# Moving the transposes of q, k and the attention output from TensorE to the DMA crossbar, from the tenth pair of heads on

## The chip, the cores and the metric

The kernel runs on one core of one Trainium2 chip. The metric is the device time of one execution in microseconds. Several executions of each kernel are timed beside executions of the kernel before on the same chip. Each "profile" is the trace of one execution ("span" is its length inside the core, about 2 us less than its device time).

Words used below: the TensorE clock of a window is the share of full speed that the trace shows as granted. The DMA share is the sum of the packets' times over the time of the core's 16 DMA engines; it can pass 1. SP's queue issues most transfers of the mid-run. SBUF holds the program's tiles; PSUM is the memory that it gives TensorE to write to.

## The reference, cut to what matters

```python
# attention: q, k, v are (8 batches, 8 heads, 576 tokens, 64), s is (8, 8, 576)
scores = q @ k.T / 8
cum    = cumsum(max(s, 0))
scores = where(causal, -1e9, scores + min(-(cum_i - cum_j), 0))
x      = softmax(scores) @ v               # heads joined: (4608 tokens, 512)
# feed-forward
h   = x @ w_in                             # (4608, 2048)
out = (h * clip(h + 3, 0, 6) / 6) @ w_out  # (4608, 512)
```

## The kernel before

Work goes by *pairs* of heads: 32 pairs, four to a batch. For each pair q and k are loaded, cast to 16 bits by GpSimd and turned, so that the 64 head dimensions lie on the partitions. TensorE does this with an identity matrix, into PSUM; VectorE copies q out, ScalarE copies k:

```python
def transpose(p, i):                       # i = 0: q, 1: k
    ...
    for e in range(6):
        nc.tensor.transpose(pt[:, 96*e : 96*(e+1)], tok[:, i, e]..., ident[0:96, 0:96])
    copy = (nc.vector.tensor_copy, nc.scalar.copy)[i]
    for hh in range(2):
        copy(out=qk[0:64, hh, i, 0:SEQ]..., in_=pt[64*hh : 64*hh + 64, 0:SEQ]...)

def transpose_x(p):                        # the attention output, for the feed-forward part
    ...
    for t in range(5):
        nc.tensor.transpose(pt[:, 128*t : 128*(t+1)], x[:, t]..., ident)
    nc.vector.tensor_copy(out=xT[:, hp, b*SEQ : (b+1)*SEQ], in_=pt[:, 0:SEQ])
    x_done[0] = p + 1                      # readiness, at build time
```

The program fixes at build time in which order each engine gets its instructions. Between the pieces of a pair's attention the program puts *groups* of four feed-forward matmuls, so that TensorE has work while ScalarE computes exponentials. A pair has eight such slots. What goes into a slot is decided when the program is built: a group of the first matmul (`m1`) may stand there only if its block's batch is ready, a group of the second (`m2`) only with some distance to the first.

```python
def m1_ready():
    return (512 * m1_list[done[1]][0] + 511) // SEQ < x_done[0] // PPB      # cut
def m2_ready():
    ...
    return done[1] >= max(need + 2, i + LAG)                               # LAG = 14
...
scores(p, 0, 0); transpose(p + 1, 0); group()                              # pair p > 4
scores(p, 0, 1); av(p - 1, 1, 0);     group()
scores(p, 0, 2); av(p - 1, 1, 1); norm(p - 1, 1); group()
corner(p); transpose(p + 1, 1);       group()
scores(p, 1, 0);                      group()
scores(p, 1, 1); av(p, 0, 0); transpose_x(p - 1); group()
scores(p, 1, 2);                      group()
av(p, 0, 1); norm(p, 0);              group()
```

The groups left over follow after the last pair (the tail).

The softmax here doesn't subtract the row's maximum and nothing guards it: scores larger than these inputs give would overflow.

## Time and profile before

| | kernel before |
|---|---|
| median of three runs | 394.0 us (391.74 to 394.42) |
| span of the profiled run | 391.0 us |
| TensorE busy | 92% |
| VectorE, ScalarE, GpSimd busy | 65%, 64%, 33% |

In mid-run TensorE's busy time equals the window's length, so its queue is the clock of the kernel there; the other figures only say who has room. The prediction shows these lines.

### The profile page before, as it was taken

The page shows a single profiled execution, that of the slowest core. Times are in us where ns is not written, and L with a number is a line of the kernel's source. Part 1 is how long each engine was busy: PE and PEld are TensorE (multiplying, and loading weights), DVE is VectorE, ACT ScalarE, POOL GpSimd, SP SyncE. Part 2 cuts the span into 40 slices and gives each one's busy share as a digit, 9 for nine tenths or more (in the row PEclk, how much of TensorE's full clock was granted, in tenths as well). Part 3 has the DMA queues.
Part 4 walks back from the last instruction along what each step waited for, and adds up shares of the span by engine and source line. Part 5 has one row for each costly group of instructions (what it writes and reads, how often), then busy time and mean ns, then how long its engine had stood idle before and what let it go on. Part 6 is the DMA issues. An engine that isn't in the chain of part 4 may idle for free.

```text
span 391.0 us, 8380 instructions
## 1 busy us (share of the span) xinstructions
PE 361.5 (92%) x3232; PEld 209.8 (54%) x3232; DVE 256.0 (65%) x518; ACT 249.6 (64%) x437; POOL 130.1 (33%) x218
## 2 busy tenths in 40 slices
PE   1576888899999999999999999999999999999995
PEld 0465555555555555555555555555555544444442
DVE  8557798667776777677767777777677555454441
ACT  5567789767777777777777777777677633433410
POOL 6777876433333333333333333333320000000000
PEclk9998999989999999999999999999999999999999
DMA  7799999904555554444555445364000001101012
GB/s 176 141 237 231 234 226 228 207 11 113 121 123 119 122 121 121 119 122 121 122 120 121 121 119 121 102 139 120 32 29 29 27 29 38 43 29 54 29 54 80
DMA packets 63744, 43.50 MB, mean 111 GB/s; under 512 B 42128, under 2 KB 58784, under 8 KB 63704
## 3 DMA queue, kind: packets, MB, share of 16 engines
q1 hardware_dynamic: 56792, 37.63, 39.5%
q0 software_dynamic: 6272, 4.78, 7.7%
q10 hardware_dynamic: 640, 0.56, 0.5%
q8 instruction: 25, 0.41, 0.5%
q14 instruction: 15, 0.12, 0.1%
HBM read 37.11 MB, written 9.44 MB: 119 GB/s over the span
## 4 chain that ended last, share of the span: by engine, by line
PE 81%; DVE 8%; ACT 4%; DMA 2%; issue 2%; POOL 1%; SPq 1%; POOLq 0%; DVEq 0%
PE po L343 30%; PE ph L323 28%; PE O L268 7%; PE S L226 6%; PE pt L194 4%; PE S L221 3%; DVE gT L332 2%; PE ptx L305 2%; DMA raw<-in_q_dram 2%; ACT tr L331 2%; DVE qk L202 1%; ACT qk L202 1%; DVE P L236 1%; DVE x L291 1%; ACT P L234 1%
## 5 line engine op out<-in xcount | busy, mean ns | idle before, releaser
L332 DVE SCALAR_TENSOR_TENSOR gT<-tr,ph 128x512 f16<-128x512 f32 x144 | 98.8, 686 | 104.3 <-ACT tr L331 104.2
L331 ACT ACTIVATE tr<-ph,bias 128x512 f32<-128x512 f32 x144 | 99.1, 688 | 93.8 <-PE ph L323 92.7
L323 PE MATMUL ph<-xT,w_in_sb 128*128 128x512 f16 x576 | 149.9, 381 | 0.8 <-DVE xT L310 0.8
L343 PE MATMUL po<-w_out_sb,gT 128*128 128x512 f16 x576 | 145.5, 379 | 0.0
L234 ACT ACTIVATE P<-S 128x512 f16<-128x512 f32 x192 | 109.6, 593 | 20.8 <-PE S L226 13.7
L343 PEld LDWEIGHTS <-gT 128*128 128x128 f16 x576 | 51.9, 97 | 46.5
L323 PEld LDWEIGHTS <-w_in_sb 128*128 128x128 f16 x576 | 49.9, 98 | 42.2 <-issue 0.8
L121 POOL DMA_DIRECT2D qk<-aug x62 | 36.5, 590 | 87.8 <-PE S L226 78.1
L167 POOL CAST tok<-raw 96x768 f16<-96x768 f32 x63 | 52.2, 864 | 1.7 <-DMA raw<-in_q_dram 0.8
L226 PE MATMUL S<-qk 68*128 68x448 f16 (+3 forms) x256 | 51.9, 285 | 0.1
L268 PE MATMUL O<-va,P 128*128 128x65 f16 x896 | 49.7, 197 | 2.0 <-DVE x L291 2.0
L202 DVE COPY qk<-pt 64x576 f16<-64x576 f16 x64 | 48.1, 751 | 4.2 <-PE pt L194 3.7
L268 PEld LDWEIGHTS <-P 128*128 128x128 f16 x896 | 41.4, 100 | 16.2 <-DVE x L291 3.4
L194 PE MATMUL pt<-ident,tok 96*128 96x96 f16 x384 | 28.6, 214 | 16.7 <-POOL tok L167 13.3
L202 ACT COPY qk<-pt 64x576 f16<-64x576 f16 x64 | 40.5, 633 | 3.4 <-PE pt L194 2.5
L173 POOL CAST va<-vraw 128x512 f16<-128x512 f32 x32 | 19.6, 613 | 66.8 <-PE O L268 56.2
L226 PEld LDWEIGHTS <-qk 68*128 68x128 f16 x256 | 24.7, 102 | 26.5 <-issue 3.2
L291 DVE TENSOR_TENSOR x<-O,rl 128x320 f16<-128x320 f32 x64 | 31.5, 491 | 2.2
L236 DVE TENSOR_TENSOR P<-P,masks_sb 128x512 f16<-128x512 f16 x64 | 29.2, 456 | 5.1 <-ACT P L234 5.0
L194 PEld LDWEIGHTS <-tok 96*128 96x128 f16 x384 | 21.8, 102 | 18.6 <-POOL tok L167 14.5
L352 DVE TENSOR_SCALAR ob<-po 128x512 f32<-128x512 f32 x36 | 24.8, 690 | 10.2 <-PE po L343 9.5
L221 PE MATMUL S<-qk 128*128 128x128 f16 x256 | 26.1, 227 | 3.6 <-DMA qk<-aug 3.6
(37 smaller groups left out, 159.1 us busy)
## 6 DMA issues: line engine op xcount, KB each, us to landing
raw<-in_q_dram SPq DMA_DIRECT2D x32, 288.0 KB, 4.5
out_dram<-ob SPq DMA_DIRECT2D x36, 256.0 KB, 2.1
raw<-in_k_dram SPq DMA_DIRECT2D x31, 288.0 KB, 4.7
vraw<-in_v_dram SPq DMA_DIRECT2D x64, 128.0 KB, 4.2
w_in_sb<-in_moe_w_in_dram POOLq DMA_DIRECT2D x4, 512.0 KB, 9.9
w_out_sb<-in_moe_w_out_dram POOLq DMA_DIRECT2D x8, 256.0 KB, 9.0
vraw<-in_v_dram SPq DMA_DIRECT2D x32, 32.0 KB, 3.9
qk<-aug POOLq DMA_DIRECT2D x62, 9.0 KB, 3.8
```

The source lines that it names most:

```text
L121: eng.dma_start(out=qks[p % NQK][64:68, hh, :, 0:SEQ], in_=aug[g : g + 1, :, :, :])
L167: eng(out=tok[:, i].rearrange("p t h d -> p h t d"), in_=raws[p % NRAW][:, i])
L194: nc.tensor.transpose(pt[:, 96 * e : 96 * (e + 1)], tok[:, i, e].rearrange("p h d -> p (h d)"), ident[0:96, 0:96],)
L202: copy(out=qk[0:64, hh, i, 0:SEQ].rearrange("p (t e) -> p t e", e=6), in_=pt[r : r + 64, 0:SEQ].rearrange("p (e t) -> p t e", e=6),)
L221: mm(S[:, c], lhsT=kT[:, c], rhs=qT[:, c], start=(j == 0), stop=(j == 3))
L226: mm(S[:, c : c + w], lhsT=kT[0:68, 128 * j : 128 * (j + 1)], rhs=qT[0:68, 128 * (j + 1) : SEQ], start=(c == 0), stop=(c != 0),)
L234: nc.scalar.activation(out=pt[:, c], in_=S, func=AF.Exp, scale=0.125)
L268: mm(o[:, i, :], lhsT=lhsT, rhs=va[:, hh, j, 0:65], **kw)
L323: mm(ph, lhsT=w_in_sb[:, kc, ft * 128 : (ft + 1) * 128], rhs=xT[:, kc, n * 512 : (n + 1) * 512], start=(kc == 0), stop=(kc == NKC - 1),)
L331: nc.scalar.activation(out=tr, in_=ph, func=AF.Relu, bias=bias3[:, 0:1])
L332: nc.vector.scalar_tensor_tensor(out=gTs[n][:, ft, :], in0=tr, scalar=6.0, in1=ph, op0=ALU.min, op1=ALU.mult)
L343: mm(po, lhsT=gTs[n][:, ft, t4 * 128 : (t4 + 1) * 128], rhs=w_out_sb[:, ft, :], start=(ft == 0), stop=(ft == NFT - 1),)
```

## The change

From pair 9 on (pairs are counted from 0), q and k of a pair are transposed by the DMA crossbar, which turns blocks of 128x128 on their way from SBUF to SBUF, out of one 16-bit tile; the attention outputs of pairs 8 to 30 go the same way straight into the feed-forward part's input. TensorE loses the transposes, and the copies out of PSUM go too. For that q and k are loaded 128 tokens to a column of blocks (rows of 256 bytes), and the second head's tokens stand 64 columns on, because 576 tokens are 4.5 blocks of 128. Four VectorE copies per pair spread the transposed blocks over the two heads. Casts and crossbar run one pair further ahead, and a batch's readiness is set nearly one pair later, to give the output time to land.

```diff
+    NPE = 2 * PPB + 1                     # 9: the first pair by the crossbar
...
+    def crossbar_qk(p):
+        J[p] = work.tile([128, 9, 128], F16, tag="jt", name="jt")
+        nc.sync.dma_start_transpose(out=J[p], in_=toks[p])
+    def spread(p, i):                     # two VectorE copies, 64x768 and 64x512
+        ...
+    def crossbar_x(p):
+        nc.sync.dma_start_transpose(out=xT[:, hp, b*SEQ : b*SEQ + 640]..., in_=X.pop(p)...)
...
     for p in range(NP):
+        if NPE <= p + 2 < NP:
+            cast_qk(p + 2, ...)
+            crossbar_qk(p + 2)
...
-            transpose(p + 1, 0)
+            get(0)                        # spread from pair 9 on
...
+        if p > NPE:
+            x_done[0] = p - 1
         scores(p, 1, 0)
...
-            transpose_x(p - 1)
+            (crossbar_x if p >= NPE else transpose_x)(p - 1)
```

More of the change, by code (lines that the diff above doesn't have):

```diff
@@ L42 @@
     NBLK = NT // 512
-    SPAD = 640
+    SPAD = 768
+    NPE = 2 * PPB + 1
     NQK = 3
@@ L77, in keep @@
         return made if n > 1 else made[0]
-    raws = keep("raw", [96, 2, 2, 6, D], F32, NRAW)
+    raws = keep("raw", [128, 24 * D], F32, NRAW)
     vraws = keep("vraw", [128, 2, 5, D], F32, NRAW)
@@ L86 @@
     PCs = keep("PC", [128, 192], F16, 2)
-    xT = keep("xT", [128, NKC, NT], F16)
+    xT = keep("xT", [128, NKC, NT + 64], F16)
     w_in_sb = keep("w_in_sb", [128, NKC, DFF], F16)
@@ L94, with raw6, raw9 @@
     aug = keep("aug", [NHEADS, 4, 2, SEQ], F16)
+    def raw6(p):
+        return raws[p % NRAW][0:96].rearrange("p (i h e d) -> p i h e d", i=2, h=2, e=6)
+    def raw9(p):
+        return raws[p % NRAW][:, 0 : 18 * D].rearrange("p (i t d) -> p i t d", i=2, t=9)
     def load_qk(p, i, eng):
         b, h0 = p // PPB, 2 * (p % PPB)
-        raw, src = raws[p % NRAW], (q, k)[i]
-        eng.dma_start(
-            out=raw[:, i].rearrange("p h e d -> p h (e d)"),
-            in_=src[b, h0 : h0 + 2].rearrange("h (p e) d -> p h (e d)", e=6),
-        )
+        src = (q, k)[i][b, h0 : h0 + 2]
+        if p < NPE:
+            eng.dma_start(
+                out=raw6(p)[:, i].rearrange("p h e d -> p h (e d)"),
+                in_=src.rearrange("h (p e) d -> p h (e d)", e=6),
+            )
+        else:
+            eng.dma_start(
+                out=raw9(p)[:, i],
+                in_=src.rearrange("h s d -> (h s) d").rearrange(
+                    "(t p) d -> p t d", p=128
+                ),
+            )
     def load_v(p, eng):
@@ L121, in load_aug @@
             eng.dma_start(
-                out=qks[p % NQK][64:68, hh, :, 0:SEQ], in_=aug[g : g + 1, :, :, :]
+                out=qks[p % NQK][64:68, hh, :, 64 * hh : 64 * hh + SEQ],
+                in_=aug[g : g + 1, :, :, :],
             )
@@ L163, in cast_qk @@
     def cast_qk(p, eng_q, eng_k):
-        tok = work.tile([96, 2, 6, 2, D], F16, tag="tok", name="tok")
+        tok = work.tile([128, 24 * D], F16, tag="tok", name="tok")
+        if p < NPE:
+            tok = tok[0:96].rearrange("p (i e h d) -> p i e h d", i=2, e=6, h=2)
+            for i, eng in enumerate((eng_q, eng_k)):
+                eng(out=tok[:, i].rearrange("p t h d -> p h t d"), in_=raw6(p)[:, i])
+        else:
+            tok = tok[:, 0 : 18 * D]
+            for i, eng in enumerate((eng_q, eng_k)):
+                eng(
+                    out=tok[:, 9 * D * i : 9 * D * (i + 1)],
+                    in_=raws[p % NRAW][:, 9 * D * i : 9 * D * (i + 1)],
+                )
         toks[p] = tok
-        for i, eng in enumerate((eng_q, eng_k)):
-            eng(
-                out=tok[:, i].rearrange("p t h d -> p h t d"), in_=raws[p % NRAW][:, i]
-            )
     def cast_v(p):
@@ L186, in t_bank @@
         if early[0] and other:
-            return psum.tile([128, SPAD], F16, tag="po", bufs=2, name=name)
-        return psum.tile([128, SPAD], F16, tag="t", name=name)
+            return psum.tile([128, 640], F16, tag="po", bufs=2, name=name)
+        return psum.tile([128, 640], F16, tag="t", name=name)
     def transpose(p, i):
@@ L202, in transpose @@
             copy(
-                out=qk[0:64, hh, i, 0:SEQ].rearrange("p (t e) -> p t e", e=6),
+                out=qk[0:64, hh, i, r : r + SEQ].rearrange("p (t e) -> p t e", e=6),
                 in_=pt[r : r + 64, 0:SEQ].rearrange("p (e t) -> p t e", e=6),
+            )
+    J = {}
+    def crossbar_qk(p):
+        J[p] = work.tile([128, 9, 128], F16, tag="jt", name="jt")
+        nc.sync.dma_start_transpose(out=J[p], in_=toks[p])
+    def spread(p, i):
+        jt, qk = J[p], qks[p % NQK]
+        for par, n in ((0, 3), (1, 2)):
+            c = 9 * i + par
+            r, sl = 64 * (c % 2), c // 2
+            src = jt[r : r + 64, sl : sl + n, :]
+            ap = [list(x) for x in src.ap]
+            ap.insert(1, [256, 2])
+            nc.vector.tensor_copy(
+                out=qk[0:64, :, i, 128 * par : 128 * par + 256 * n].rearrange(
+                    "p h (s two c) -> p h s two c", two=2, c=128
+                )[:, :, :, 0, :],
+                in_=bass.AP(src.tensor, src.offset, ap),
             )
@@ L209, with qk_of @@
     mm = nc.tensor.matmul
+    def qk_of(p, hh):
+        r = 64 * hh
+        return (qks[p % NQK][:, hh, i, r : r + 640] for i in range(2))
     def Pof(p, hh):
@@ L214, in scores @@
     def scores(p, hh, g):
-        qT, kT = qks[p % NQK][:, hh, 0], qks[p % NQK][:, hh, 1]
+        qT, kT = qk_of(p, hh)
         pt = Pof(p, hh)
@@ L242, in corner @@
         for hh in range(2):
-            qT, kT = qks[p % NQK][:, hh, 0], qks[p % NQK][:, hh, 1]
+            qT, kT = qk_of(p, hh)
             mm(
@@ L313, in transpose_x @@
         x_done[0] = p + 1
+    def crossbar_x(p):
+        b, hp = p // PPB, p % PPB
+        nc.sync.dma_start_transpose(
+            out=xT[:, hp, b * SEQ : b * SEQ + 640].rearrange("p (t c) -> p t c", c=128),
+            in_=X.pop(p).rearrange("p t h d -> p (t h d)"),
+        )
     gTs, pos = {}, {}
@@ L411 @@
     for i in range(NQK):
-        nc.vector.memset(qks[i][0:64, :, :, SEQ:SPAD], 0.0)
+        for hh in range(2):
+            r = SEQ + 64 * hh
+            nc.vector.memset(qks[i][0:64, hh, :, r : r + 64], 0.0)
     for t in Ps:
@@ L422 @@
             copy(
-                out=qks[i][64:128, hh].rearrange("p i (t c) -> p i t c", c=128),
+                out=qks[i][64:128, hh, :, 64 * hh : 64 * hh + 640].rearrange(
+                    "p i (t c) -> p i t c", c=128
+                ),
                 in_=stair_sb[64:128, :, None, :].to_broadcast([64, 2, 5, 128]),
@@ L465 @@
         nxt = p + 1 < NP
+        ahead = NPE <= p + 2 < NP
+        if p and p + 1 < NPE:
+            cast_qk(p + 1, nc.gpsimd.tensor_copy, nc.gpsimd.tensor_copy)
+        if ahead:
+            cast_qk(p + 2, nc.gpsimd.tensor_copy, nc.gpsimd.tensor_copy)
+            crossbar_qk(p + 2)
         if p and nxt:
-            cast_qk(p + 1, nc.gpsimd.tensor_copy, nc.gpsimd.tensor_copy)
             cast_v(p + 1)
@@ L471, with get @@
         next_weights(1 if p < 3 else 2 if p < 4 else 3)
+        for m in (p + 3, p + 4):
+            if m < NP and (m < NPE) == (m == p + 3):
+                for i in range(2):
+                    load_qk(m, i, nc.sync)
         if p + 3 < NP:
-            for i in range(2):
-                load_qk(p + 3, i, nc.sync)
             load_v(p + 3, nc.sync)
+        def get(i):
+            if p + 1 < NPE:
+                transpose(p + 1, i)
+            elif nxt:
+                spread(p + 1, i)
         if p < PPB:
@@ L479 @@
             scores(p, 0, 1)
-            if nxt:
-                transpose(p + 1, 0)
+            get(0)
             scores(p, 0, 2)
@@ L488 @@
             scores(p, 1, 0)
-            transpose(p + 1, 1)
+            get(1)
             scores(p, 1, 1)
@@ L507 @@
             scores(p, 0, 2)
-            transpose(p + 1, 0)
+            get(0)
             group()
@@ L512 @@
             scores(p, 0, 0)
-            if nxt:
-                transpose(p + 1, 0)
+            get(0)
             group()
@@ L523 @@
         corner(p)
-        if nxt:
-            transpose(p + 1, 1)
+        get(1)
         group()
+        if p > NPE:
+            x_done[0] = p - 1
         scores(p, 1, 0)
```

## The prediction

> **What bounds the kernel now.** I first read the page's busy shares and slices, then a table of windows, the PE timeline inside one pair, the costliest groups, and the waits of the SP queue.
>
> ```profile
> PE 361.5 (92%) x3232; PEld 209.8 (54%) x3232; DVE 256.0 (65%) x518; ACT 249.6 (64%) x437; POOL 130.1 (33%) x218
> PE   1576888899999999999999999999999999999995
> PEclk9998999989999999999999999999999999999999
> DMA  7799999904555554444555445364000001101012
> ```
>
> TensorE leads. DMA is full in slices 3 to 8, up to about 78 us, then half busy to about 275 us. TensorE's granted clock dips near 80 us. The windows (busy us, then clock, DMA share, GB/s) put numbers on this.
>
> ```profile
> 150.90:191.30 40.40, 40.24 (x390) 23.82 (x389) 28.54 (x61) 29.20 (x52) 14.50 (x24) 1.00 0.47 117
> 305.00:390.00 85.00, 81.97 (x436) 38.27 (x433) 39.02 (x64) 30.22 (x46) 0.00 (x0) 1.00 0.12 44
> 77.50:80.00 2.50, 1.88 (x18) 1.07 (x17) 0.95 (x4) 2.16 (x4) 0.00 (x0) 0.82 0.15 29
> 80.00:82.50 2.50, 2.50 (x14) 1.24 (x13) 1.07 (x4) 1.18 (x2) 1.10 (x2) 0.50 0.00 0
> ```
>
> The first is four pairs (one batch), 10.10 us per pair: columns are TensorE, its weight loads, VectorE, ScalarE, GpSimd. TensorE is busy 40.24 of 40.40 us, VectorE 71%, ScalarE 72%. What TensorE is spared here is time, as long as nobody else becomes slower than it. The last two rows are pair 8, where the order of the program offers no feed-forward matmuls for some slots: TensorE idles a little, and then runs at half clock for 2.5 us.
>
> The timeline of TensorE (start, length, line) shows what a transpose costs there:
>
> ```profile
> 163.77 0.42 PE L194 MATMUL pt<-ident,tok 96*128 96x96 f16 x6
> 164.03 1.03 PE L343 MATMUL po<-w_out_sb,gT 128*128 128x512 f16 x4
> 167.58 0.42 PE L194 MATMUL pt<-ident,tok 96*128 96x96 f16 x6
> 167.83 1.03 PE L323 MATMUL ph<-xT,w_in_sb 128*128 128x512 f16 x4
> 170.25 0.45 PE L305 MATMUL ptx<-ident,x 128*128 128x128 f16 x5
> 170.54 1.03 PE L323 MATMUL ph<-xT,w_in_sb 128*128 128x512 f16 x4
> ```
>
> Matmuls overlap, so the start of the next group counts, not the length: six transposes of q take 0.26 us, six of k 0.25, five of the attention output 0.29. Together 0.80 us per pair, 8% of it.
>
> ```profile
> L202 DVE COPY qk<-pt 64x576 f16<-64x576 f16 x64 | 48.1, 751 | 4.2 <-PE pt L194 3.7
> L202 ACT COPY qk<-pt 64x576 f16<-64x576 f16 x64 | 40.5, 633 | 3.4 <-PE pt L194 2.5
> L310 DVE COPY xT<-ptx 128x576 f16<-128x576 f16 x32 | 14.5, 452 | 1.0 <-PE ptx L305 0.9
> L422 DVE COPY qk<-stair_sb 64x1280 f16<-64x1280 f16 x2 | 2.0, 1018 | 0.4 <-DMA stair_sb<-stair 0.4
> SPq L354 <- DVE ob L352: 230.6, 35, 12.0
> ```
>
> The first three copies go away; the fourth has the form of the new ones. The last line is a wait: the SP queue spends 230.6 us blocked, in order, on the store of the result. It has time to spare, but what stands behind that store waits with it.
>
> **What the Trainium skill says.** "VectorE: DVE Perf Modes", section "The three transpose paths", gives 390 ns for a 128x128 transpose on TensorE and 1309 ns for one by the DMA crossbar. The trace disagrees on the first for a filled pipeline: 0.29 us for five is 58 ns each. So the change trades little TensorE time for much DMA time; it pays only because TensorE is the bound one. "DMA: Bandwidth & Descriptors", section "Latency and other measured facts", has 261 GB/s for a crossbar transpose in one kernel; the trace before holds none. The same page, section "Issuing engines are not separate DMA queues", says that all DMAs share the 16 engines: the 0.47 share is where the crossbar must fit. "Advanced Engine Details and Errata", section "X-Bar Transpose (TRN2)", warns of two transpose streams at once; here all come from SP, so one stream.
>
> **The change part by part.**
> *TensorE.* Pairs 9 to 31 lose their q and k transposes, and the outputs of pairs 8 to 30 theirs: 23 of each. 23 x 0.80 = 18.4 us off the path. Span 391.0 becomes 372.6; the pair goes from 10.10 to 9.30 us.
> *ScalarE.* Loses 2 x 0.633 = 1.27 us per pair: 7.30 - 1.27 = 6.03 of 9.30 us. Not on the path.
> *VectorE.* Loses 2 x 0.751 + 0.452 = 1.95 us. It gains four copies inside SBUF, two of 64x768 and two of 64x512 elements (the second head's tokens included, as the crossbar's chunks are common to both). The stair copy takes 1018 ns for 1280 elements in runs of 128; with about 155 ns fixed (a 128-column mask costs 0.22 us in the timeline, a 512-column one 0.42) it is 0.67 ns per element: 0.67 and 0.50 us, together 2.34. VectorE: 7.13 - 1.95 + 2.34 = 7.5 of 9.30 us, 81%. Not the bound, but with less slack than 71%.
> *GpSimd.* Casts 128x576 in place of 96x768, so shorter; 33% busy; not on the path.
> *DMA.* In 150 to 232 us the trace's packets are, per pair: 1152 of 256 bytes (v) at 23 ns, 384 of 1536 bytes (q, k) at 89 ns, 128 of 2048 bytes (results) at 92 ns. Over 16 engines 1.68 + 2.13 + 0.73 = 4.5 us, the 0.47 of the window. New q and k loads are rows of 256 bytes: 2304 x 23 / 16 = 3.36 us, 1.2 us more. The crossbar moves 9 + 5 blocks of 128x128, 459 KB per pair: at the skill's 261 GB/s an estimate of 1.8 us. Sum 4.5 + 1.2 + 1.8 = 7.5 us of 9.30: 81%. It fits, without much room.
> *Order.* q and k of pair p+2 are now transposed at the top of pair p, so a spread has about 8 us from issue to use. For the output the change sets the readiness of a batch almost one pair later. Followed through the program's order: until pair 11 nothing differs; then the feed-forward work that is ready runs out, and seven slots at the end of pair 12 and in pair 13 stay empty. From pair 14 all 8 are filled again, and the tail does 87 groups in place of 80. The work itself is only moved (a group costs 0.86 us anywhere), but the hole costs what pair 8's does: that pair ran from 73.4 to 82.8 us, 9.3 us, with three groups; its matmul work at full clock is 10.1 - 5 x 0.86 = 5.8 us, so 3.5 us were lost, about half of it to the lower clock. I take 3 us for the new hole, and give back 1 us in pair 8, where TensorE waited for copies of transposes (0.80 and 0.62 us) that are gone.
> *Start.* The crossbar for pair 9 is issued while the DMA engines are still full (slices to 78 us), with one more pair of loads ahead of it. I take 1.5 us of lateness there and 1 us in sum where a batch's first feed-forward block meets its last transposed output.
> Sum: 391.0 - 18.4 + 3 - 1 + 1.5 + 1 = 377.1 us of span, 13.9 less; from the median of 394.0, 380 us.
>
> **The rivals.**
> *DMA becomes the bound.* For it: the loads get 1.2 us longer, and the skill's 1309 ns times 14 is 18 us per pair if blocks do not overlap. Against it: the skill's 261 GB/s, and 1309 ns for a lone block must hold much that is latency. The room is 9.3 - 5.7 = 3.6 us per pair; a crossbar at under 459 KB / 3.6 us = 127 GB/s ends the gain, and at half of that the pair lasts about 13 us and the kernel 391 + 23 x 3 = 460 us.
> *The SP queue or late transposed data become the wait.* SP is in order: transposes wait for casts and for the normalised output, and stores of results wait behind them. If issuing a transpose takes some us, or an output comes late at each batch's start, TensorE stands still some us for each of five batches, and its clock drops after each: 385 to 395 us. For it: SP already waits 230.6 us on the result's store. Against it: that is slack, and use lies most of a pair behind issue.
> *VectorE.* If the new copies run at one element per cycle (the 751 ns copy has 1.04 ns per element beyond its fixed part), they cost 3.3 us and VectorE is at 8.5 of 9.3 us; TensorE would wait here and there, some 0.2 us per pair: 384 us.
>
> **Range and chances.** The 18.4 us are sure, being counted from the timeline; with no hole at all the time would be 375. What is unsure is the crossbar's speed, which no row before shows. About two in three that nothing new binds (375 to 386), one in five that waits eat over half of the gain, one in seven that DMA or SP binds and the kernel is slower. So 380 us, 374 to 396 for 8 in 10; faster 0.66, same 0.20, slower 0.14.
>
> **What would show it.** A step is right if: the pair in mid-run lasts 9.3 us with TensorE near 99%; the new copies last about 0.67 and 0.50 us; 256-byte load packets stay near 23 ns and the DMA share is near 0.8; the slot hole appears in pairs 12 and 13 with a lower clock behind it; the tail starts earlier and has 87 groups. It is wrong if TensorE waits on the spread copies or on DMA in every pair, or if the DMA share stands at 1 past 100 us: then the crossbar's packets were slower than I took them.

## More of the kernel before

One more page line of before is needed for comparison, the count of DMA packets:

```profile
DMA packets 63744, 43.50 MB, mean 111 GB/s; under 512 B 42128, under 2 KB 58784, under 8 KB 63704
```

## The result, and the profile after

The changed kernel took 375.81 us (median of four, 374.26 to 376.71), against 393.86 us (four runs, 391.74 to 394.42). The ratio is 0.955, with a 95% interval of 0.950 to 0.960. Ratios here are the mean time of one kernel's runs over the mean of the other's in the same rounds, so not quite the quotient of the medians. Executions over 1.5% slower than the fastest of the same kernel are left out of the means.

The page of the changed kernel, the same lines as the prediction shows of before:

```profile
PE 343.6 (92%) x2841; PEld 192.5 (52%) x2841; DVE 243.8 (65%) x544; ACT 225.3 (60%) x391; POOL 122.8 (33%) x218
PEclk9997699999999999999999999999999999999999
DMA  8699999999979799979999989798411001010012
DMA packets 150589, 54.01 MB, mean 145 GB/s; under 512 B 137808, under 2 KB 145632, under 8 KB 150552
```

TensorE has 18 us less to do (361.5 to 343.6) and its share of the span is the same 92%: still the bound. The DMA line is what looks dangerous. Half busy in mid-run before, it is now at nine tenths to the end of the attention, with well over twice the packets. The windows by stage (four pairs; the pair with empty slots; pair 8; columns as in the prediction):

```profile
160.59:197.48 36.89, 36.89 (x321) 20.65 (x320) 26.15 (x65) 25.13 (x44) 12.62 (x24) 1.00 0.96 170
116.90:123.70 6.80, 5.59 (x67) 3.34 (x64) 5.69 (x13) 5.48 (x10) 4.99 (x9) 1.00 1.12 195
74.42:81.76 7.34, 5.84 (x66) 3.62 (x65) 5.24 (x13) 4.61 (x9) 4.65 (x9) 1.00 1.39 169
```

In mid-run TensorE is busy in all of 36.89 us, four pairs of 9.22. VectorE is busy 26.15 of 36.89 us, 71%, the same share as before. In pair 13 TensorE idles 1.2 us, and unlike pair 8 of before its clock stays at 1.00. The new operations, and the SP queue's wait:

```profile
L249 DVE COPY qk<-jt 64x768 f16<-64x768 f16 x46 | 17.3, 375 | 0.7
L249 DVE COPY qk<-jt 64x512 f16<-64x512 f16 x46 | 13.2, 287 | 1.0
jt<-tok SPq DMA_TRANSPOSE x23, 3.5
xT<-x SPq DMA_TRANSPOSE x23, 3.4
SPq L415 <- DVE ob L413: 117.2, 33, 8.4
```

The copies take 375 and 287 ns, and VectorE is hardly ever idle ahead of them (0.7 and 1.0 us in 92 copies), so the transposed q and k are there when wanted. A transpose lands 3.4 to 3.5 us after its issue (medians). SP's wait for the result's store fell from 230.6 to 117.2 us, while the issuing of its transfers grew from 119 to 212 us: the slack pays for issuing the transposes.

For a ledger I take the start of each pair, the first score matmul of its first head, from TensorE's timeline of the two traces:

| stage | before, us | after, us | difference | of which |
|---|---|---|---|---|
| to the start of pair 8 | 73.43 | 74.42 | +0.99 | open, see below |
| pair 8 | 9.33 | 7.34 | -1.99 | -0.51 transposes, -1.48 less idling, clock stays up |
| pairs 9 to 11 | 30.05 | 27.67 | -2.38 | 3 x 0.80 transposes |
| pairs 12 and 13 | 20.36 | 14.27 | -6.09 | -1.60 transposes, -6.05 seven groups moved to the tail, -0.32 batch start, +1.88 hole |
| pairs 14 to 30 | 171.60 | 156.78 | -14.82 | -13.60 transposes, -1.28 four batch starts |
| pair 31 and tail | 86.23 | 93.12 | +6.89 | +6.05 seven groups, -0.29 transposes, +1.06 a wait |
| span | 391.00 | 373.60 | -17.40 | |

A group is 0.864 us (four matmuls in the timeline), so pair 13 with its three groups should have taken 9.22 - 5 x 0.864 = 4.90 us; it took 6.77, and that is the 1.88 (with rounding). The first pair of each later batch lasted 10.34 us before, the others 10.02; now all last 9.22.

The first two rows are not settled. Pair 8 began at 73.4 and 73.3 us in the two traces with the start of before (the other is readiness alone, below), and at 74.0 to 75.6 us in nine traces with the changed start (left out: two with a long mask operation, see the copies, and the crossbar from pair 5 on). So the lateness may well belong to the change. But the crossbar is not all of it: the nine were already late at the start of pair 7 (64.2 to 65.6 us, against 64.0 and 63.9), where the first transpose is issued, and the latest of all, at 75.6 us, has q and k on TensorE throughout. The cause stays open. Nor is pair 8's gain steady: the kernel with readiness at once, whose program is the changed one up to there, took 8.67 us for it, at a clock of 0.80. At the start of pair 9 before stood at 82.8 us, the changed kernel at 81.8 and, in its second trace, at 82.3.

### The profile page after: what moved, and what is told of

Its sections match the earlier page's. It is cut to its first block, busy times and chain, and to the rows that moved or that the text cites. A ratio compares the mean times of both kernels' runs of the same rounds, so it can differ in the third digit from the quotient of the medians.

```text
span 373.6 us, 7629 instructions
## 1 busy us (share of the span) xinstructions
PE 343.6 (92%) x2841; PEld 192.5 (52%) x2841; DVE 243.8 (65%) x544; ACT 225.3 (60%) x391; POOL 122.8 (33%) x218
## 3 DMA queue, kind: packets, MB, share of 16 engines
q1 hardware_dynamic: 143640, 48.19, 65.6%
## 4 chain that ended last, share of the span: by engine, by line
PE 83%; DVE 9%; ACT 2%; DMA 2%; issue 2%; POOL 1%; SPq 1%; POOLq 0%; DVEq 0%; ACTq 0%
PE po L404 33%; PE ph L384 30%; PE O L321 7%; PE S L279 7%; PE S L274 3%; DMA raw<-in_q_dram 2%; DVE qk L226 2%; DVE gT L393 1%; PE pt L218 1%; ACT tr L392 1%; ACT P L287 1%; DVE P L289 1%; DVE x L344 1%; DVE qk L249 1%; PE ptx L358 1%
## 5 line engine op out<-in xcount | busy, mean ns | idle before, releaser
L384 PE MATMUL ph<-xT,w_in_sb 128*128 128x512 f16 x576 | 148.3, 379 | 0.1
L287 ACT ACTIVATE P<-S 128x512 f16<-128x512 f32 x192 | 112.1, 595 | 45.1 <-PE S L274 22.5
L404 PEld LDWEIGHTS <-gT 128*128 128x128 f16 x576 | 50.3, 98 | 46.1
L384 PEld LDWEIGHTS <-w_in_sb 128*128 128x128 f16 x576 | 51.2, 98 | 43.9 <-issue 0.4
L197 POOL CAST va<-vraw 128x512 f16<-128x512 f32 x32 | 19.7, 615 | 57.2 <-PE O L321 48.2
L189 POOL CAST tok<-raw 128x576 f16<-128x576 f32 x46 | 30.1, 677 | 11.7 <-DMA jt<-tok 4.1
L249 DVE COPY qk<-jt 64x768 f16<-64x768 f16 x92 | 30.5, 331 | 1.7
L274 PEld LDWEIGHTS <-qk 128*128 128x128 f16 x256 | 20.0, 102 | 16.9 <-issue 4.7
L218 PE MATMUL pt<-ident,tok 96*128 96x96 f16 x108 | 9.6, 242 | 15.5 <-POOL tok L185 12.9
L218 PEld LDWEIGHTS <-tok 96*128 96x128 f16 x108 | 7.6, 119 | 17.3 <-POOL tok L185 14.1
```

The source lines that it names most:

```text
L249: nc.vector.tensor_copy(out=qk[0:64, :, i, 128 * par : 128 * par + 256 * n].rearrange("p h (s two c) -> p h s two c", two=2, c=128)[:, :, ...
L274: mm(S[:, c], lhsT=kT[:, c], rhs=qT[:, c], start=(j == 0), stop=(j == 3))
L287: nc.scalar.activation(out=pt[:, c], in_=S, func=AF.Exp, scale=0.125)
L384: mm(ph, lhsT=w_in_sb[:, kc, ft * 128 : (ft + 1) * 128], rhs=xT[:, kc, n * 512 : (n + 1) * 512], start=(kc == 0), stop=(kc == NKC - 1),)
L404: mm(po, lhsT=gTs[n][:, ft, t4 * 128 : (t4 + 1) * 128], rhs=w_out_sb[:, ft, :], start=(ft == 0), stop=(ft == NFT - 1),)
```

## The experiments

**Theory.** TensorE's queue sets the pace of pairs 9 to 30; the gain is its own time for the transposes, less what the later readiness costs in slots that stay empty. **Rivals.** The gain is the relief of VectorE and ScalarE from copies; the DMA is now at its limit; the later readiness costs more, or is not needed. Twelve kernels were run, in three series. The kernel before had medians of 395.49 us in the first, 392.56 in the second and 393.30 in the third. All results were correct.

### TensorE's time alone, given back

The change with as many transposes of a constant tile on TensorE as there were, never read.

```diff
                 spread(p + 1, i)
+                fake(i)                   # 6 x nc.tensor.transpose(pt, masks[0:96, ...], ident)
...
             (crossbar_x if p >= NPE else transpose_x)(p - 1)
+            fake_x()                      # 5 x nc.tensor.transpose(pt, masks[:, ...], ident)
```

> The change, with TensorE transposing a constant tile as often as it transposed before (6 + 6 + 5 per pair, into PSUM that nobody reads), so only TensorE's time is given back; result unchanged. TensorE theory: mid-run pair back to 10.0 us, 375.8 + 18.4 = 394 us. Rival (relief of VectorE and ScalarE is the gain): under 380 us.

Measured: 392.60 us, ratio 0.9995 (0.993 to 1.006): the gain is gone, to within the interval's 2.5 us, with everything else of the change still in place. A window of four pairs:

```profile
146.98:187.04 40.06, 40.06 (x389) 23.80 (x388) 26.23 (x65) 25.10 (x44) 13.23 (x25) 1.00 1.00 163
```

10.02 us a pair, the pace of before, though VectorE and ScalarE (26.23 and 25.10 us) have only the changed kernel's work.

### The copies alone, given back

The five removed copies run again, in the same form and from PSUM, into scratch, on VectorE and ScalarE.

```diff
+                copy = (nc.vector.tensor_copy, nc.scalar.copy)[i]
+                for hh in range(2):
+                    copy(out=junk[:, i, :]..., in_=keep_pt[0][r : r + 64, 0:SEQ]...)
...
+                nc.vector.tensor_copy(out=junkx, in_=keep_pt[0][:, 0:SEQ])
```

> The change, with the five removed copies out of PSUM executed again on VectorE (2 x 0.75 + 0.45 us per pair) and ScalarE (2 x 0.63) into scratch from pair 9 on, beside the new ones; result unchanged. TensorE theory: VectorE goes from 71% to 92% of a pair and TensorE still sets the pace: 376 to 379 us, pair 9.2 to 9.3 us. Rival: VectorE's time counts, pair 10 us or more, 390 us or more.

Measured: 380.87 us, ratio 0.970 (0.964 to 0.976): 5 us slower than the change, more than the theory's 3 at most, far from the rival's 14 or more. The traces say where (a mid-run window, then TensorE's timeline in pair 13):

```profile
131.19:187.00 55.81, 55.81 (x482) 31.37 (x481) 48.53 (x113) 43.20 (x78) 19.36 (x36) 0.99 0.87 173
126.46 0.42 PE L324 MATMUL O<-va,P 128*128 128x65 f16 x8 [1.67 <-DVE x L347]
127.71 0.38 PE L282 MATMUL S<-qk 68*128 68x320 f16 x2 [0.83 <-ACT P L290]
```

With VectorE at 48.53 of 55.81 us, 87%, TensorE is still busy throughout; pairs 15 to 30 last 9.24 us in place of 9.22. But pair 13 lasts 10.39 us in place of 6.77, at a clock of 0.87: with three feed-forward groups in place of eight there is little to hide VectorE's and ScalarE's work, and TensorE waits for it in the open. So the copies (1.95 us of VectorE, 1.27 of ScalarE a pair) cost 0.02 us a pair from pair 15 on, where the slots are full (0.16 to 0.28 in pairs 9 to 12), and 3.6 us in pair 13, where they are empty; which of the two engines costs it is not told apart. (This trace also holds a pair 6 of 10.80 us, ahead of any changed instruction; a mask operation on VectorE took 1.85 us in it in place of some 0.4. Its cause was not looked for.)

### The two halves of the change, and the readiness alone

q and k only (output by TensorE, readiness at once); output only; and the kernel before with the later readiness.

```diff
 # q and k only
-        if p > NPE:
-            x_done[0] = p - 1
-            (crossbar_x if p >= NPE else transpose_x)(p - 1)
+            transpose_x(p - 1)
 # output only
-    NPE = 2 * PPB + 1
+    NPE = NP                              # q and k always by TensorE
+    NPX = 2 * PPB + 1                     # the output by the crossbar from pair 9
 # readiness only (on the kernel before)
-        x_done[0] = p + 1
+        if p < 8 or p == NP - 1:
+            x_done[0] = p + 1
...
+        if p > 9:
+            x_done[0] = p - 1
```

> The change with the crossbar for q and k alone; the attention output is transposed on TensorE as before and readiness is set at once. If the gain is the TensorE time of the transposes (first theory): 23 x 0.51 us saved = 11.7, and pair 8 about 1.2 us shorter as in the full change; no slots left empty in pairs 12 and 13: 381 us, mid-run pair 9.5 us. If the gain comes from relieving VectorE and ScalarE of the q and k copies (rival): all of it stays, 376 us.

> The crossbar for the attention output alone, from pair 9 on, with the later readiness. TensorE theory: 23 x 0.29 = 6.7 us saved, 1.3 us more at the batch starts (four pairs of 10.34 us become 10.02), against 2 to 3.5 us for the empty slots of pairs 12 and 13: 388 to 390 us. Rival (the copies matter): no gain over the delay alone, 394 us or more.

> The kernel before with nothing but the later readiness of a batch (one pair later from pair 10 on), all transposes on TensorE. If the empty slots cost what the traces show in pair 13 and the batch starts gain 4 x 0.32 us: 394 + 2 to 3.5 - 1.3 = 395 to 396 us, pairs of 10.34 us gone. If readiness is free: 394 us or less.

| kernel | median, us | ratio (95% interval) | mid-run pair, us | pairs 12 and 13, us |
|---|---|---|---|---|
| before | 395.49 | 1 | 10.02 (10.34) | 10.34, 10.02 |
| q and k only | 380.69 | 0.966 (0.959 to 0.973) | 9.50 (9.56) | 9.57, 9.50 |
| output only | 391.96 | 0.996 (0.988 to 1.004) | 9.74 | 8.02, 9.88 |
| readiness only | 397.36 | 1.010 (1.002 to 1.019) | 10.02 | 8.30, 8.81 |
| the change (its own four runs, before 393.86) | 375.81 | 0.955 (0.950 to 0.960) | 9.22 | 7.50, 6.77 |

In brackets the first pair of a batch. The pairs shorten by 0.52 us for q and k and 0.28 for the output, within a hundredth of what the timeline of before gave (0.51 and 0.29). The 10.34 us pairs vanish with the later readiness, whoever transposes; with q and k alone moved, at once ready, 0.06 us of the 0.32 is left. But the later readiness alone makes the kernel about 1% slower. Here are pair 13 of the readiness-only kernel and pair 13 of the output-only kernel, as windows, with one line of the latter's timeline:

```profile
121.01:129.82 8.81, 6.31 (x83) 4.17 (x80) 6.12 (x12) 6.40 (x12) 5.23 (x9) 1.00 0.19 32
```

```profile
121.03:130.91 9.88, 7.54 (x79) 4.52 (x76) 5.87 (x11) 6.51 (x12) 5.94 (x9) 0.83 0.48 109
125.28 0.41 PE L219 MATMUL pt<-ident,tok 96*128 96x96 f16 x6 [2.35 <-DVE qk L227]
```

With all transposes on TensorE the hole costs 8.81 - (10.02 - 5 x 0.864) = 3.1 us; with q and k on TensorE and the output on the crossbar 9.88 - (9.74 - 4.32) = 4.5 us, part of it a lower clock (0.83). In the changed kernel it costs 1.9, since nothing waits there for copies of transposes. The kernel with TensorE's time given back bears this out: its transposes are there, their copies are not, and pair 13 lasts 7.04 us, a hole of 1.3. So the output half alone was worth less than I expected (388 to 390 us), and the crossbar for q and k makes the hole cheaper that the output's readiness opens. In total times the two halves add up to the whole within the intervals.

### The readiness at once, and one slot later

The change with a batch ready as soon as the output's transpose is issued; and one slot after that. The change itself ran again beside the second.

```diff
-        if p > NPE:
-            x_done[0] = p - 1
...
             (crossbar_x if p >= NPE else transpose_x)(p - 1)
+            x_done[0] = p                 # at once
         group()
+        if p >= NPE:
+            x_done[0] = p                 # or here: one slot later
```

> The change with readiness set as soon as the crossbar of the attention output is issued. If the delay is needed: the first feed-forward block of five batches waits on TensorE for a transfer that takes 3.4 us to land plus its issue, 4 to 5 us each, against 1.9 us won as no slots stay empty: about 394 to 398 us. If the data come in time anyway: 374 us.

> The change, with a batch ready one slot after its last output's crossbar transpose is issued, in place of nearly one pair later. In the run with no delay TensorE waited only 0.3 to 0.4 us of transfer per batch start, and the empty slots were gone; one slot is 1.1 us of other matmuls. If the hole in pair 13 (1.9 us) is lost for the reason given and nothing waits: 1.9 us less than the change, 374 us, no wait on the transposed output, pairs 12 and 13 without idle TensorE. If the batch starts wait all the same: 376 us.

> The change itself once more, as the base for the other three on this chip: 0.955 of the kernel before, about 375.8 us where that has 393.9.

At once: 375.63 us, ratio 0.954 (0.947 to 0.961), the same as the change. I had expected waits of 4 to 5 us for five batches. TensorE's waits and its timeline in pair 16 show how short they are:

```profile
PE ph L384 <- DMA xT<-x: 1.7, 5, 0.4
154.46 0.81 PE L384 MATMUL ph<-xT,w_in_sb 128*128 128x512 f16 x3
155.60 0.38 PE L384 MATMUL ph<-xT,w_in_sb 128*128 128x512 f16 x1 [0.33 <-DMA xT<-x]
```

Only the fourth matmul of a group needs the last pair's output. SP issued its transpose at 152.95 us, 2.3 us ahead of where TensorE stopped, and it came 2.65 us after the issue began. The batch's first pair lasts 9.70 us in place of 9.22, five times 0.5 us, about what the absent hole and the absent wait in the tail give back (pair 13 lasts 9.23 with all eight groups).

One slot later: 374.10 us, ratio 0.9505 (0.947 to 0.954), against 375.45 us and 0.953 (0.950 to 0.956) for the change in the same rounds. No wait on the output is left in its trace and mid-run pairs last 9.22. Pairs 12 and 13 hold 15 groups in 18.37 us, where 2 x 9.22 - 0.86 = 17.58 would be ideal: 0.8 us of hole is left of 1.9. The direction and size fit, but the intervals overlap; this is the fastest kernel by 1.35 us in medians, not by a proven margin.

### How much room the DMA has

The change with the crossbar transpose of q and k issued once more, and twice more, into scratch.

```diff
         nc.sync.dma_start_transpose(out=J[p], in_=toks[p])
+        j2 = work.tile([128, 9, 128], F16, tag="jt2", bufs=1, name="jt2")
+        nc.sync.dma_start_transpose(out=j2, in_=toks[p])
+        # second kernel: and 8 blocks into a third tile
```

> The change, with the crossbar transpose of q and k issued a second time into scratch: 1152 packets of 256 bytes more, at 24.5 ns over 16 engines 1.76 us of DMA per pair. The mid-run DMA share of 0.96 would become 1.15; the kernel before shows shares of 1.2 in its full start, so there should be room: at most 2 us more, 378 us. If 0.96 already is the limit: 1.76 us more per pair, 375.8 + 40 = 416 us.

> The same with two extra transposes (9 and 8 blocks): 3.3 us of DMA more per pair, a share of 1.32 where 1.2 is the most seen. Now DMA should set the pace: pair 9.22 x 1.32 / 1.2 = 10.1 us, 375.8 + 21 = 397 us, and TensorE waits on the spread copies. If there is still room: under 380 us.

Once more: 384.79 us, ratio 0.978 (0.972 to 0.984), 9 us more than the change where I had expected at most 2. Twice more: 422.70 us, ratio 1.072 (1.063 to 1.080), 47 us more where I had expected 21. Windows of one and the other, and a wait of each:

```profile
193.70:232.80 39.10, 37.12 (x323) 20.66 (x321) 27.05 (x65) 25.10 (x44) 13.37 (x24) 1.00 1.10 198
201.42 0.38 PE L386 MATMUL ph<-xT,w_in_sb 128*128 128x512 f16 x1 [1.98 <-DMA xT<-x]
```

```profile
167.96:230.09 62.13, 50.70 (x402) 27.27 (x400) 33.78 (x81) 31.37 (x55) 19.13 (x34) 0.89 1.13 197
PE ph L388 <- DMA xT<-x: 28.8, 5, 8.2
```

Overloaded, the DMA engines show a share of 1.10 and 1.13 and 197 to 198 GB/s, not the 1.2 and 227 GB/s that the start of before reached with its larger packets. The changed kernel stands at 0.96. So the room is some 0.15 of a pair, about 1.4 us, and one more transpose of an estimated 1.76 us uses it up. Where it shows was a surprise too: three of four pairs still last 9.22 us, and the lateness is paid in one piece at the batch's start, where a feed-forward block waits for the last output (in the second kernel up to 8.2 us, after which the clock drops: pairs of 16 to 19.7 us). In the first kernel three of five batches wait, and pair 13 alone, 12.05 us in place of 6.77, is over half of its loss. The average from pair 17 to 28 is (270.93 - 156.88) / 12 = 9.50 and (302.21 - 167.96) / 12 = 11.19 us. The limit is averaged over a batch, I take it because buffers reach two pairs ahead; that was not tested.

The limit need not be the DMA engines: SP's queue ran out at the same time. Its issues one after the other, in the second kernel:

```profile
169.25 1.38 SPq L241 DMA_TRANSPOSE jt<-tok  x1
170.68 1.63 SPq L243 DMA_TRANSPOSE jt<-tok  x1
172.36 0.71 SPq L114 DMA_DIRECT2D raw<-in_q_dram  x1
```

From pair 17 to 28 issuing took SP 2.8 of 10.10 us a pair before, 6.9 of 9.22 in the changed kernel, 8.9 of 9.50 and 10.5 of 11.19 with the extra transposes. The changed kernel's SP still stands idle for 2.1 us a pair in gaps over 0.2 us, that of the other two for less than 0.1. A transpose of nine blocks took SP at least 1.24 us in any run. So a busy queue would explain why the engines stay below the 1.2 seen elsewhere. Whether SP's own work sets the pace, or its issues lengthen because the engines are behind, these runs do not tell apart.

### Filling the holes, and starting earlier

The one-slot kernel with a looser rule for second-matmul groups, so that pair 8 gets seven groups; and the change from pair 5 on in place of 9.

```diff
 # fill
+        if not m1_ready():
+            return done[1] >= need
         return done[1] >= max(need + 2, i + LAG)
-    LAG = 14
+    LAG = 4
 # earlier
-    NPE = 2 * PPB + 1
+    NPE = PPB + 1
```

> The same, and second-matmul groups may run without the lag of 14 when no first-matmul group is ready (lag 4 otherwise), so pair 8 gets 7 groups in place of 3. If the idle time and half clock of pair 8 (2.4 us in the change's trace) are for want of feed-forward matmuls: another 2 us, 371 to 372 us. If pair 8 waits for data that the groups need: 374 us or more.

> The change with the crossbar from the sixth pair on in place of the tenth. The DMA engines are full until about 65 us and pairs 5 to 8 last 7.8 us with only 4 groups each, not bound by TensorE, so the 4 x 0.80 us of transposes saved should bring little; the later readiness adds its empty slots to those that pair 8 has already. Theory: 376 to 382 us, with waits on the crossbar or late loads between pairs 4 and 9. Rival (every pair moved gains alike): 372.6 us.

Filled: 385.33 us, ratio 0.978 (0.974 to 0.982), a clear miss. Pair 8 did what was hoped: seven groups in 9.50 us, where the one-slot kernel needed 6.96 for three, so four groups of 0.864 us cost 2.5 us. But the looser rule moves all later groups, and with them the stores of results. Pair 12, on the SP queue and on TensorE:

```profile
118.00 0.61 SPq L129 DMA_DIRECT2D vraw<-in_v_dram  x1
119.87 0.36 SPq L415 DMA_DIRECT2D out_dram<-ob  x1
120.28 1.26 SPq L371 DMA_TRANSPOSE xT<-x  x1
```

```profile
123.71 0.58 PE L384 MATMUL ph<-xT,w_in_sb 128*128 128x512 f16 x1 [2.39 <-DMA xT<-x]
```

SP stands from 118.6 to 119.9 us before a store whose data are not computed yet, with the output's transpose behind it; TensorE then waits 2.39 us for that transpose, and 3.32 us in pair 20. Pairs 12 and 13 last 11.88 and 10.39 us. I take this to be what the change's later readiness protects against: it does not matter in the order of groups that readiness at once produces, where the transpose is issued in good time, and it does in this one. Pair 6 also lasted 11.38 us in this trace, with a mask operation of 1.58 us as in the copies' experiment, so part of the 11 us stays open.

Earlier: 389.36 us, ratio 0.988 (0.984 to 0.992): 14 us slower than the change, worse than the 376 to 382 of the theory and far from the rival's 372.6. Pair 5 lasts 15.77 us. VectorE's and TensorE's timelines:

```profile
60.59 0.68 DVE L249 COPY qk<-jt 64x768 f16<-64x768 f16 x2 [6.78 <-DMA jt<-tok]
```

```profile
62.67 0.62 PE L321 MATMUL O<-va,P 128*128 128x65 f16 x8 [7.28 <-DVE x L344]
```

The crossbar came 6.8 us late while the DMA engines were full (a share of 1.31 in pair 5) and SP was issuing all the time (15.2 of the pair's 15.8 us; one transpose took it 4.97 us). VectorE stood at the spread with the attention's normalisation behind it, and TensorE behind that. The empty slots moved too: pairs 8 and 9 last 4.20 and 15.40 us, the latter with a wait of 3.35 us for an output's transpose and TensorE at a clock of 0.58. So of the two starts tried the tenth pair is the better; by then the loads have caught up (the DMA line of before falls at about 78 us). Others were not tried.

## Why the prediction was right or wrong

The time, 375.8 us, lies in the range of 374 to 396, near its lower end, and 4 us under the 380 predicted. The reason it gave was the right one; several of its terms were not. Part was luck: the transposes' cost in DMA was half as much again as estimated, and they just fitted; and the clock, which the prediction named as a sign, did not drop behind the hole.

- **TensorE, 18.4 us: right.** The pair went to 9.22 us (9.30 predicted from the average of 10.10, which holds the longer batch starts). Giving TensorE's time back alone took the whole gain (ratio 0.9995).
- **ScalarE and VectorE off the path: right in mid-run, with VectorE's term mis-sized.** The copies take 375 and 287 ns, not 670 and 500: VectorE is at 71%, not 81%. I had scaled from one copy at the start. The two new forms differ by 88 ns for 256 elements, 0.34 ns per element, where copies out of PSUM take 1.04 by the prediction's own reckoning. The Trainium skill says as much: "VectorE: DVE Perf Modes", section "Rules for kernel authors", promises four times the rate for dense bf16 copies inside SBUF; these are of another 16-bit type, and the trace agrees roughly, with three times the rate per element of the copies out of PSUM.
- **DMA: it fits, but the crossbar's term was too small.** Loads were right: 256-byte packets average 24.2 ns between 150 and 232 us, 23 predicted. In the trace's packet records there are about 5,220 of them a pair; 1152 for v, 2304 for q and k and 1792 for the 14 blocks are 5,248, so the crossbar moves in them too. At that average it takes an estimated 1792 x 24.2 / 16 = 2.7 us, not 1.8, and the share is 0.96, not 0.81. The prediction's own sign of slow crossbar packets, a share of 1 past 100 us, was thus all but met. One pair's headroom is some 1.4 us, and SP's 2.1: the rivals of a DMA or SP bound were nearer than the one in seven that I gave them suggests, and one more transpose made one of them true. Of SP I had counted the waiting alone; issuing takes it 6.9 us a pair, 4 more than before.
- **The hole in pairs 12 and 13: right in place, 1.9 us in place of 3.** I took pair 8 of before as its model, but half of that loss was clock, which this hole does not lose, and part was waiting for copies of transposes, which are gone. Pair 8 gained 1.5 us beyond its transposes in this trace, for 1 predicted; with readiness at once it gained 0.2.
- **Lateness at the start, 1.5 us: about the size, not where I put it.** VectorE hardly waits for the data of a spread copy. The start comes 1 us later in this trace, 0.6 to 2.2 us later in the nine with the changed start, but part of that stands there before the first crossbar transpose, for a cause that stays open. The mechanism is real: four pairs earlier it costs 7 us.
- **Batch starts, 1 us lost: wrong in sign.** I took the average of four pairs and missed that the first pair of a batch was 0.32 us longer; TensorE waited there for the copy of the last output, 0.8 us in the five batches. The later readiness removes the 0.32 in each, a gain of 1.6 us.
- **The tail: not foreseen.** TensorE waits 1.06 us in the last pair for a normalisation. The same wait stands in the readiness-only and output-only traces and in none with readiness at once.

The measured terms, -18.4 + 1.9 - 1.5 + 1.0 - 1.6 + 1.1 = -17.5, give the span's 17.4; I had -18.4 + 3 - 1 + 1.5 + 1 = -13.9. The 3.5 us between are three terms that erred to the same side (1.1 in the hole, 0.5 in pair 8, 2.6 at the batch starts) and 0.5 at the start, against 1.1 for the tail.

## What to carry to other kernels

If one engine is busy in all of a window, moving work off it is worth that work's spacing in its timeline (0.05 us a transpose here, not the 0.2 us of its record), as long as the engine that takes it, and the queue that issues to it, have room. Measure that room by loading it further: the estimate of 1.8 us a pair for the crossbar was a third too low, and the queue's issue time was in no term of the sum. A change in what is ready when moves every slot that follows, stores in an in-order queue included: count the empty slots, and look at what stands ahead of the transfer that somebody waits for. Idle time of other engines is free only while there is other work to hide it.

## What the Trainium skill lacked or had wrong

- "VectorE: DVE Perf Modes", "The three transpose paths": 390 ns for a TensorE transpose of 128x128. In a filled pipeline five took 0.29 us, 58 ns each, and six of 96x96 took 0.26 us. The page has no figure for that case, which decides whether moving them pays; the skill's page on TensorE has one for plain matmuls in a row, but none for transposes in a row.
- The same table: 1309 ns per block by the DMA crossbar. Nine blocks in one transpose landed 3.5 us after issue, 0.39 us a block with all latency in it. The table does not say how blocks of one transfer overlap.
- "DMA: Bandwidth & Descriptors", "Latency and other measured facts": 261 GB/s for a crossbar transpose. Beside loads in 256-byte rows, 459 KB a pair took an estimated 2.7 us of all engines, some 170 GB/s.
- No page that I found says what a transpose from SBUF to SBUF costs the issuing queue on this chip: in the changed kernel at least 1.26 us on SP for nine blocks and 1.20 us for five.
